# A static order for one TensorE-bound program laid out again, with other transfer constants and one more wait in its planner

## The chip, the cores and the metric

The kernel runs on one core of a Trainium2 chip. The metric is the device time in microseconds (us) of one execution; the kernel before has a median of 942.45 us over three runs (941.67 to 943.02). Five engines run their own instruction lists in order: TensorE (PE), VectorE (DVE), ScalarE (ACT), GpSimd (POOL) and SyncE (SP, which here only issues transfers).

## What is computed

Random-feature attention over 8 batches, 8 heads, 576 positions and 64 channels with 128 features, followed by a layer norm and a two-layer perceptron (512 to 2048 to 512) with a residual:

```python
def phi(x):
    proj = np.einsum('bhsd,md->bhsm', x, omega)
    h = proj - np.sum(x * x, axis=-1, keepdims=True) / 2.0
    return np.exp(h - np.max(h, axis=-1, keepdims=True)) / np.sqrt(m)
q_p, k_p = phi(q * scale), phi(k * scale)
kv = np.einsum('bhsm,bhsd->bhmd', k_p, v)
z = np.sum(k_p, axis=2)
x = np.einsum('bhsm,bhmd->bhsd', q_p, kv) / (np.einsum('bhsm,bhm->bhs', q_p, z)[..., None] + 1e-06)
# x as rows of 512, then
xn = (x - mu) / np.sqrt(var + 1e-06) * g_ln
out = x + np.maximum(xn @ w_ch1, 0.0) @ w_ch2
```

## The kernel before

**Tiles.** The 8 x 576 positions are 4608 rows, cut into 36 chunks of 128 rows (`c`) and 9 tiles of 512 rows (`t`, four chunks each). Tiles 0 to 2 go through the perceptron plainly: `mm1` (L1085 to L1087) makes one of 16 blocks `f` of the hidden layer, `relu` evicts it into a high and a low part, `mm2` (L1128 to L1130) adds it to four result banks. Each product is three matmuls, high by high, low by high and high by low. Tiles 3 to 8 are three pairs `p`. For a pair the first layer is done with seven products instead of eight on quarters of the operands: `one_set` (L1429 to L1431) makes two blocks of the hidden layer for both tiles in seven products; between them ACT copies a partial sum from bank to bank (`gen_copy`, L1486) or into `hid` (`gen_snap`, L1492), and DVE adds (L1499, L1507). After two sets `one_chunk` (L1748 to L1750) does the second layer for eight chunks, and DVE drains each result bank into `x` (`drain`, L1767). In the last pair the second layer has seven products too (`two_chunks`, `product2`, L1668 to L1670); their operands are made by `form_a11`, `form_a21`, `form_a12`, `form_s4` and `form_sum`.

**Attention** runs in the gaps of that stream as short visits on PE: `gen_k` (L663, features of keys), `gen_sums` (L726, keys by values), `gen_q` (L824, and L841/L842 from chunk 8 on, features of queries), `gen_x` (L907, the output). For a query chunk from 8 on, SP loads `qD` (L829), ACT makes the high part (L834), DVE the low part (L836), PE multiplies (L841, L842), ACT or DVE copies out (L369, L371), POOL takes the maximum over partitions (L853), DVE subtracts it (L858), ACT takes the exponential (L861). For keys, `gen_v` loads `v` and DVE sets its column of ones when it has landed (L622). A chunk of `x` is normalised (L991 or L993), split into halves (L1008), transposed by a transfer (L1011) and copied in place (L369 or L371). `gen_rs` makes the row scale of a tile from its statistics with small instructions on DVE (L963, L971 to L977) and ACT (L967, L969).

**Order.** Nothing is decided on the chip. At build time `Plan.run` picks the next piece of work for each engine by its own estimate of when it can start, and by rank; the order in which it picks is the order in which each engine's instructions are written. Its estimates rest on constants: a transfer lands `FLIGHT` (1.8 us) after its issue or after the one ahead of it, whichever is later, plus its bytes at 400 GB/s; a transposing transfer (`"flip"`) takes `FLOWN` more; `MARGIN` is added to what ACT or DVE take over from another engine; during the first part of a maximum on POOL, DVE instructions marked `"two"` (two operands in SBUF) are held back from `EDGE[0]` before to `EDGE[1]` after a window of 1.9 us. `EDGE` and `MARGIN` count only after `TILL` (60 us). `SHIFT` moves the rank of single pieces, `WAIT` and `SOLO` say when a lone visit is let onto PE, `EARLIER`, `WF`, `W2F` set base ranks. Semaphores for every true dependence are put in by the framework, whatever the order.

In the last pair, bank `b_b` is read twice: by ACT, and then DVE, in `form_a12` (L1595, L1597), and by DVE in `form_s4` (L1609).

Of the kernel before, what the change touches and what calls it, by code (L numbers as in the profile page):

```python
# [1957 lines left out]
```

## Time and profile before

| | |
|---|---|
| median of 3 runs | 942.45 us |
| the profiled execution | 943.46 us |
| its span, first to last instruction | 941.7 us |
| PE busy | 925.3 us (98%) |
| DVE busy | 677.3 us (72%) |
| ACT busy | 503.4 us (53%) |
| POOL busy | 123.3 us (13%) |
| granted TensorE clock | 1.0 throughout |
| DMA queues, share of 16 engines | 65%, 215 GB/s on average |

The profiled execution took 943.46 us; 1.8 us of it lie outside the span, and it is 1.0 us above the median. A timeline row has start, duration, engine, line, operation and tiles; in brackets stands how long the engine was idle ahead of it, and what ended that. A row such as `DMA quad<-qD` among the waits means that the engine waited for a transfer's landing.

### The profile page before, as it was taken

The numbers are of one execution on the slowest core, as the hardware profiler recorded it, in microseconds if no ns is written. First come the engines' busy times: TensorE is split into PE (matmuls) and PEld (weight loads), VectorE is DVE, ScalarE is ACT, GpSimd is POOL, SyncE is SP. The second block draws the span as 40 slices with busy tenths as digits, with TensorE's granted clock in tenths as the row PEclk, the third lists the DMA queues.
The fourth block names the chain that finished last, engine by engine and source line by source line (L and its number), as shares of the span: only waits on it lengthen the run. The fifth ranks groups of instructions, "written<-read, shape, count | busy, mean of one in ns | idle before, by whom it ended". The sixth has DMA issues, their size and how long they took to land.

```text
span 941.7 us, 17585 instructions
## 1 busy us (share of the span) xinstructions
PE 925.3 (98%) x6863; PEld 767.1 (81%) x6863; DVE 677.3 (72%) x1176; ACT 503.4 (53%) x919; POOL 123.3 (13%) x47
## 2 busy tenths in 40 slices
PE   8999999999999999999999999999999999999998
PEld 6887778788888878887787888887888888989988
DVE  6999999565588865546664668797837496585765
ACT  6888886454665654334545556656513245263442
POOL 5002304100303350000410111404000000000000
PEclk9999999999999999999999999999999999999999
DMA  8576599964456955575766664695937468484562
GB/s 306 203 264 230 162 332 397 340 203 131 143 184 205 202 144 203 181 261 176 245 152 208 171 211 156 218 379 124 330 120 260 168 214 303 163 293 125 189 224 90
DMA packets 142579, 202.72 MB, mean 215 GB/s; under 512 B 44064, under 2 KB 79008, under 8 KB 142496
## 3 DMA queue, kind: packets, MB, share of 16 engines
q1 hardware_dynamic: 142352, 201.34, 65.0%
q8 instruction: 54, 0.88, 0.4%
q10 hardware_dynamic: 144, 0.26, 0.1%
q14 instruction: 29, 0.24, 0.1%
HBM read 140.74 MB, written 52.43 MB: 205 GB/s over the span
## 4 chain that ended last, share of the span: by engine, by line
PE 52%; DMA 6%; DVE 4%; ACT 2%; issue 1%; SPq 0%; DVEq 0%; ACTq 0%
PE b L1429 7%; PE b L1431 7%; PE b L1430 7%; PE b L1748 5%; PE b L1750 5%; PE b L1749 5%; PE b L1668 2%; PE b L1670 2%; PE b L1669 2%; DMA quad<-qD 2%; PE b L726 1%; PE b L907 1%; PE b L663 1%; PE b L1130 1%; PE b L1128 1%
## 5 line engine op out<-in xcount | busy, mean ns | idle before, releaser
L853 POOL PARTITION_ALL_REDUCE quad<-quad x34 | 117.1, 3463 | 528.6 <-ACT quad L369 321.3
L1429 PE MATMUL b<-w,w 128*128 128x512 f32 x336 | 132.2, 393 | 1.8 <-ACT hid L1492 1.0
L1430 PE MATMUL b<-w,w 128*128 128x512 f32 x336 | 130.8, 389 | 0.0
L1431 PE MATMUL b<-w,w 128*128 128x512 f32 x336 | 130.8, 389 | 0.0
L1748 PE MATMUL b<-w,w 128*128 128x512 f32 x256 | 101.5, 396 | 1.1 <-DVE x L1767 1.1
L1750 PE MATMUL b<-w,w 128*128 128x512 f32 x256 | 99.9, 390 | 0.9 <-DVE w L1517 0.9
L1749 PE MATMUL b<-w,w 128*128 128x512 f32 x256 | 99.8, 390 | 0.0
L672 ACT ACTIVATE kp<-b,mb 128x128 f32<-128x128 f32 x256 | 70.3, 391 | 42.3 <-DVE mb L666 40.4
L1085 PE MATMUL b<-xnT,w 128*128 128x512 f32 (+1 forms) x200 | 78.6, 393 | 0.0
L1128 PE MATMUL b<-w,hid 128*128 128x512 f32 x192 | 77.8, 405 | 0.5 <-ACT hid L1101 0.5
L1087 PE MATMUL b<-xnT,w 128*128 128x512 f32 (+1 forms) x200 | 76.4, 382 | 0.5 <-DVE xnT L1061 0.4
L1429 PEld LDWEIGHTS b<-w,w 128*128 128x128 f32 x336 | 63.0, 188 | 16.9 <-ACT b L1486 2.1
L1086 PE MATMUL b<-xnT,w 128*128 128x512 f32 (+1 forms) x200 | 76.3, 382 | 0.2 <-DVE w L580 0.2
L1130 PE MATMUL b<-w,hid 128*128 128x512 f32 x192 | 75.0, 391 | 0.0
L1129 PE MATMUL b<-w,hid 128*128 128x512 f32 x192 | 75.0, 390 | 0.0
L1431 PEld LDWEIGHTS b<-w,w 128*128 128x128 f32 x336 | 63.1, 188 | 13.3
L1492 ACT COPY hid<-b 128x512 f32<-128x512 f32 x64 | 37.6, 587 | 67.0 <-PE b L1431 37.2
L1430 PEld LDWEIGHTS b<-w,w 128*128 128x128 f32 x336 | 63.1, 188 | 12.6
L1499 DVE TENSOR_TENSOR b<-b,hid 128x512 f32<-128x512 f32 x32 | 22.3, 697 | 63.6 <-ACT hid L1492 63.6
L1486 ACT COPY b<-b 128x512 f32<-128x512 f32 x32 | 18.4, 577 | 89.4 <-PE b L1431 68.3
L1748 PEld LDWEIGHTS b<-w,w 128*128 128x128 f32 x256 | 48.0, 188 | 13.0 <-DVE x L1767 2.2
L1750 PEld LDWEIGHTS b<-w,w 128*128 128x128 f32 x256 | 48.0, 188 | 11.5 <-DVE w L1517 1.3
(224 smaller groups left out, 2045.5 us busy)
## 6 DMA issues: line engine op xcount, KB each, us to landing
w<-wf SPq DMA_DIRECT2D x168, 256.0 KB, 4.8
w<-w SPq DMA_DIRECT2D x32, 512.0 KB, 6.2
w<-w2a SPq DMA_DIRECT2D x32, 512.0 KB, 5.4
quad<-qD SPq DMA_DIRECT2D x28, 512.0 KB, 4.8
w2a<-w SPq DMA_DIRECT2D x16, 512.0 KB, 5.6
wf<-wide SPq DMA_DIRECT2D x32, 256.0 KB, 3.2
w2t<-wide SPq DMA_DIRECT2D x32, 256.0 KB, 3.9
away<-x SPq DMA_DIRECT2D x30, 256.0 KB, 3.5
```

What stands on the lines that cost most here:

```text
L853: nc.gpsimd.partition_all_reduce(mx.rearrange("p a b -> p (a b)"), qc.rearrange("p a b -> p (a b)"), P, bass_isa.ReduceOp.max)
L1085: nc.tensor.matmul(ph[:, ts], w[:, 0, cs], xnT[:, 0, k, ts], start=k + i0 == 0, stop=False)
L1086: nc.tensor.matmul(ph[:, ts], w[:, 1, cs], xnT[:, 0, k, ts], start=False, stop=False)
L1087: nc.tensor.matmul(ph[:, ts], w[:, 0, cs], xnT[:, 1, k, ts], start=False, stop=k == NK - 1 and i1 == TC)
L1128: nc.tensor.matmul(accs[i][:, c], hl[:, 0, cs], w[:, 0, c], start=(f == 0), stop=False)
L1130: nc.tensor.matmul(accs[i][:, c], hl[:, 1, cs], w[:, 0, c], start=False, stop=f == NF - 1 and c == parts[-1])
L1429: nc.tensor.matmul(o, w[:, 0, cs], hi[:, k], start=first and k == 0, stop=False, skip_group_check=True)
L1430: nc.tensor.matmul(o, w[:, 1, cs], hi[:, k], start=False, stop=False, skip_group_check=True)
L1431: nc.tensor.matmul(o, w[:, 0, cs], lo[:, k], start=False, stop=k == 1, skip_group_check=True)
L1748: nc.tensor.matmul(acc[:, o], hl[:, 0, cs], w[:, 0, o], start=n == 0 and o is parts[0], stop=False)
L1749: nc.tensor.matmul(acc[:, o], hl[:, 0, cs], w[:, 1, o], start=False, stop=False)
L1750: nc.tensor.matmul(acc[:, o], hl[:, 1, cs], w[:, 0, o], start=False, stop=n == 3 and o is parts[-1])
```

## The change

Four things in the planner and one wait. A transfer issued after 60 us is reckoned to land 0.5 us later, at 1/1.11 of the rate. `FLOWN` goes from 2.2 to 1.2, `EDGE` from (0.5, 0.2) to (0.1, 0.1), ACT's `MARGIN` from 0.15 to 0.2. `SHIFT` is another table (entries for the same kinds of pieces with other numbers), and `W2F`, `WAIT`, `SOLO`, `EARLIER`, `WF` have other values. `form_s4` waits, in the plan, until `form_a12` has issued ACT's read of the bank.

```diff
-                self.dma_at = max(self.dma_at, start + Plan.FLIGHT) + cost * (1.55 if self.dma_at < Plan.SLOW else 1.0)
+                late = start > Plan.TILL
+                self.dma_at = max(self.dma_at, start + Plan.FLIGHT + 0.5 * late) + cost * (1.55 if self.dma_at < Plan.SLOW else 1.11 if late else 1.0)
...
         nc.scalar.activation(out=hl[:, 0], in_=bank(b_b), func=AF.Relu)
+        done(("a12", j))
...
         yield wait("f", j, "S2")
+        yield wait("a12", j)
         s4 = yield from whole(j, "S4")
...
-SHIFT = {('gen_w2store', 13): 4, ('gen_q', 26): 12, ('gen_var', 28): -18, ...
+SHIFT = {('gen_var', 16): -2, ('gen_w2store', 13): 12, ('gen_q', 26): 12, ...
-W2F = -40
-WAIT = (0, 0, 24)
-SOLO = (0, 0, 0)
+W2F = -30
+WAIT = (-2, -6, 23)
+SOLO = (2, 9, 5)
...
-MARGIN = {ACT: 0.15, DVE: 0.15}
-FLOWN, EDGE = 2.2, (0.5, 0.2)
+MARGIN = {ACT: 0.2, DVE: 0.15}
+FLOWN, EDGE = 1.2, (0.1, 0.1)
...
-EARLIER = {2: 1.8, 3: 2.25, 4: 2.5, 5: 3.95, 6: 6.6, 7: 5.75, 8: 5.3}
+EARLIER = {2: 1.25, 3: 2.2, 4: 2.7, 5: 3.6, 6: 6.8, 7: 5.65, 8: 3.95}
...
-WF = (44, 12.75)
+WF = (35, 15.0)
```

PE's main stream (the three perceptron parts) stands in the same order in both programs, and so does its whole start up to the visit of `gen_sums` for batch 1 behind block 7 of tile 0. Between there and the last pair the attention's visits stand at other places of that stream; in the last pair PE, DVE and ACT have the same rows. Lines of the changed kernel are 1 to 3 higher than those of before.

**First pair, DVE.** The ones of the `v` of batch 6, chunk 2 (MEMSET on `v_`), with the maxima of two key chunks ahead (L666 TENSOR_REDUCE) and a drain behind (L1767). Before:

```order
L836 TENSOR_TENSOR quad_4619<-quad_4600,quad_4619 64x1024
L666 TENSOR_REDUCE mb_4604<-b 128x8
L666 TENSOR_REDUCE mb_4566<-b 128x8
L622 MEMSET v_4680 128x8
L1767 SCALAR_TENSOR_TENSOR x_4423<-b,st_3543,x_4423 128x512
```

Now:

```order
L667 TENSOR_REDUCE mb_4345<-b 128x8
L667 TENSOR_REDUCE mb_4331<-b 128x8
L837 TENSOR_TENSOR quad_4584<-quad_4564,quad_4584 64x1024
L837 TENSOR_TENSOR quad_4593<-quad_4581,quad_4593 64x1024
L1770 SCALAR_TENSOR_TENSOR x_4475<-b,st_2549,x_4475 128x512
L623 MEMSET v_4621 128x8
```

Two low parts of queries and a drain have moved between the maxima and the MEMSET.

**First pair, ACT.** The high part of query chunk 25 (`quad_4850` before, `quad_4746` now) and the copies of `one_set` (COPY b<-b, and COPY of `hid` at L1492, now L1493). Before:

```order
L1486 COPY b<-b 128x512
L1008 COPY wide_4868<-wide_4857 128x1024
L369 COPY quad_4866<-b 128x1024
L834 CAST quad_4850<-quad_4838 128x1024
L1492 COPY hid_4251<-b 128x512
```

Now, chunk 25 first and, some rows later, chunk 26 (`quad_4940`):

```order
L835 CAST quad_4746<-quad_4735 128x1024
L370 COPY xnT_4436<-wide_4785 128x2x4x128
L673 ACTIVATE kp_4717<-b,mb_4718 128x128 x4
L370 COPY xnT_4436<-wide_4802 128x2x4x128
L673 ACTIVATE kp_4717<-b,mb_4718 128x128 x4
```

```order
L1516 ACTIVATE w_30_4992<-b 128x512
L970 ACTIVATE w_150_4365<-w_150_4365 128x4
L835 CAST quad_4940<-quad_4930 128x1024
L1487 COPY b<-b 128x512
L862 ACTIVATE quad_4958<-quad_4958 128x1024
```

Chunk 25's CAST has moved out of the set into the chunks of the second layer; chunk 26's stands directly ahead of a copy between banks.

**Second pair, DVE.** The low parts of query chunks 34 and 35 (`quad_6534`, `quad_6545` before) and the row scale's small instructions on `st_`. Before:

```order
L836 TENSOR_TENSOR quad_6534<-quad_6513,quad_6534 64x1024
L1767 SCALAR_TENSOR_TENSOR x_6399<-b,w_150_4245,x_6399 128x512
L963 TENSOR_SCALAR st_6068<-st_6068 128x4
L971 TENSOR_TENSOR st_6068<-st_6068 128x4
L836 TENSOR_TENSOR quad_6545<-quad_6530,quad_6545 64x1024
```

Now:

```order
L964 TENSOR_SCALAR st_6115<-st_6115 128x4
L1770 SCALAR_TENSOR_TENSOR x_6391<-b,w_150_4365,x_6391 128x512
L837 TENSOR_TENSOR quad_6523<-quad_6502,quad_6523 64x1024
L837 TENSOR_TENSOR quad_6533<-quad_6519,quad_6533 64x1024
L1770 SCALAR_TENSOR_TENSOR x_6404<-b,w_150_4365,x_6404 128x512
L972 TENSOR_TENSOR st_6115<-st_6115 128x4
```

The instruction that takes ACT's result (L971, now L972) has moved behind both low parts and a drain.

**Last pair, SP.** The loads of weights into `kv` and `v` for `product2` and the loads of chunks of `x` (L945, now L946, from `away`). Before:

```order
L1651 DMA v_7715<-w2t_114 128x512
L945 DMA w_140_4228<-away_6405 128x512
L1359 DMA w_20_3550<-wf_91 128x512
L1649 DMA v_7716<-w2a_98 128x2x256
L945 DMA x_7865<-away_6748 128x512
L1359 DMA w_20_3550<-wf_92 128x512
L1649 DMA v_7717<-w2a_100 128x2x256
L945 DMA x_7878<-away_6812 128x512
```

Now:

```order
L1654 DMA v_7716<-w2t_114 128x512
L1360 DMA w_20_3554<-wf_91 128x512
L1652 DMA v_7717<-w2a_98 128x2x256
L1360 DMA w_20_3554<-wf_92 128x512
L1652 DMA v_7718<-w2a_100 128x2x256
L946 DMA x_7838<-away_6563 128x512
L946 DMA x_7852<-away_6393 128x512
L946 DMA w_140_4342<-away_6731 128x512
```

Three loads of `x` have moved behind the last load into `v`.

## Rows read from the trace of the kernel before

**Rows 1.** The page: PE's busy time, and its commonest matmul with mean duration.

```profile
PE 925.3 (98%) x6863; PEld 767.1 (81%) x6863; DVE 677.3 (72%) x1176; ACT 503.4 (53%) x919; POOL 123.3 (13%) x47
...
L1430 PE MATMUL b<-w,w 128*128 128x512 f32 x336 | 130.8, 389 | 0.0
```

**Rows 2.** PE's waits, longest first: us in total, times, longest; first and last.

```profile
PE b L841 <- DVE quad L836: 2.2, 2, 1.8
...
PE b L663 <- DVE hid L1103: 0.2, 1, 0.2
```

**Rows 3.** Waits of ACT and DVE for transfers, same columns.

```profile
ACT quad L834 <- DMA quad<-qD: 20.1, 9, 5.2
...
DVE v L622 <- DMA v<-vF: 14.1, 7, 4.6
```

**Rows 4.** Timeline, first pair, around 437 us.

```profile
431.23 0.34 SPq L618 DMA_DIRECT2D v<-vF  x1
...
436.72 0.07 DVE L622 MEMSET v<- 128x8 f32 x1 [2.55 <-DMA v<-vF]
...
437.62 0.50 PE L1748 MATMUL b<-w,w 128*128 128x512 f32 x1 [1.06 <-DVE x L1767]
```

**Rows 5.** Timeline, first pair, 451 to 462 us.

```profile
451.08 0.43 SPq L829 DMA_DIRECT2D quad<-qD  x1
...
458.15 1.05 ACT L834 CAST quad<-quad 128x1024 fp32r<-128x1024 f32 x1 [2.69 <-DMA quad<-qD]
459.11 0.58 ACT L1492 COPY hid<-b 128x512 f32<-128x512 f32 x1
...
459.74 0.50 PE L1429 MATMUL b<-w,w 128*128 128x512 f32 x1 [1.01 <-ACT hid L1492]
...
461.82 0.47 PE L841 MATMUL b<-quad,om_hi 128*128 128x512 f32 x1 [0.43 <-DVE quad L836]
```

**Rows 6.** Timeline, first pair, 465 to 469 us, while POOL takes a maximum.

```profile
465.18 0.68 DVE L1517 SCALAR_TENSOR_TENSOR w<-b,w 128x512 fp32r<-128x512 f32 x1
...
465.96 2.47 DVE L1517 SCALAR_TENSOR_TENSOR w<-hid,w 128x512 fp32r<-128x512 f32 x1
...
469.09 0.51 PE L1750 MATMUL b<-w,w 128*128 128x512 f32 x1 [0.86 <-DVE w L1517]
```

**Rows 7.** Timeline, second pair, 638 to 643 us.

```profile
638.31 1.03 ACT L834 CAST quad<-quad 128x1024 fp32r<-128x1024 f32 x1
...
640.43 0.20 ACT L969 ACTIVATE st<-st 128x4 f32<-128x4 f32 x1
...
640.67 0.16 DVE L971 TENSOR_TENSOR st<-st 128x4 f32<-128x4 f32 x1 [1.80 <-ACT st L969]
640.86 1.22 DVE L836 TENSOR_TENSOR quad<-quad,quad 64x1024 fp32r<-64x1024 f32 x1
...
642.23 0.47 PE L841 MATMUL b<-quad,om_hi 128*128 128x512 f32 x1 [1.77 <-DVE quad L836]
```

**Rows 8.** Timeline, last pair, a load into `v` and its matmul.

```profile
803.39 0.53 SPq L1649 DMA_DIRECT2D v<-w2a  x1
...
808.69 0.38 PE L1668 MATMUL b<-v,w 128*128 128x256 f32 x1 [0.43 <-DMA v<-w2a]
```

**Rows 9.** Timeline, last pair, the two readers of bank `b_b`, second of eight times.

```profile
798.99 0.60 ACT L1595 ACTIVATE w<-b 128x512 fp32r<-128x512 f32 x1 [0.76 <-PE b L1431]
...
800.80 0.68 DVE L1609 SCALAR_TENSOR_TENSOR wide<-b,wide 128x512 f32<-128x512 f32 x1
```

**Rows 10.** View of the transfers: count, median us from issue to landing.

```profile
wide<-wide SPq DMA_TRANSPOSE x32, 4.3
```

**Rows 11.** Timeline of the start: two DVE instructions and PE's first wait in the perceptron.

```profile
27.48 0.41 DVE L371 CAST w<-wide 128x512 fp32r<-128x512 f32 x1
...
32.07 0.68 DVE L564 TENSOR_TENSOR wide<-wide,g_sb 128x512 f32<-128x512 f32 x1
...
38.30 0.39 PE L1087 MATMUL b<-xnT,w 128*128 128x256 f32 x1 [0.43 <-DVE xnT L1061]
```

More of the change, by code (lines that the diff above doesn't have):

```diff
@@ L1886 @@
 MOST_URGENT = -2000
-SHIFT = {('gen_w2store', 13): 4, ('gen_q', 26): 12, ('gen_var', 28): -18, ('gen_var', 15): -30, ('gen_sums', 6, 1): 26, ('gen_q', 16): -36, ('gen_x', 26): 20, ('gen_q', 7): -8, ('gen_var', 33): 12, ('gen_q', 4): 2, ('gen_k', 3, 3): -8, ('gen_x', 7): -8, ('gen_q', 30): 28, ('gen_sums', 3, 2): -8, ('gen_x', 35): -10, ('gen_sums', 0, 2): -40, ('gen_x', 29): 2, ('gen_q', 34): 34, ('gen_q', 18): 4, ('gen_w2store', 12): -12, ('gen_wform', 5): -4, ('gen_w2store', 14): -6, ('gen_q', 33): 16, ('gen_var', 17): 16, ('gen_x', 21): -2, ('gen_q', 24): -2, ('gen_q', 14): -2, ('gen_q', 10): 0, ('gen_sums', 4, 2): -2, ('gen_x', 1): 0, ('gen_x', 15): -24, ('gen_var', 8): 12, ('gen_w2store', 2): -4, ('gen_q', 15): 4, ('gen_var', 10): 40, ('gen_x', 13): 8, ('gen_var', 7): -6, ('gen_var', 13): -32, ('gen_var', 21): 16, ('gen_x', 6): -14, ('gen_k', 3, 2): 2, ('gen_w2store', 1): 4, ('gen_x', 3): 14, ('gen_k', 2, 4): -2, ('gen_sums', 6, 2): 12, ('gen_var', 23): 4, ('gen_sums', 0, 1): -8, ('gen_sums', 0, 0): 16, ('gen_sums', 7, 1): -16, ('gen_var', 5): 4, ('gen_q', 35): 0, ('gen_q', 27): 16, ('gen_var', 3): 8, ('gen_x', 23): -8, ('gen_q', 22): 2, ('gen_w2store', 9): 2, ('gen_q', 9): 4, ('gen_k', 4, 1): 16, ('gen_var', 31): -16, ('gen_k', 5, 4): 16, ('gen_x', 31): -4, ('gen_q', 11): -16, ('gen_k', 3, 4): 8, ('gen_q', 28): 16, ('gen_k', 7, 2): 2, ('gen_var', 6): -12, ('gen_k', 6, 0): -4, ('gen_k', 6, 1): 8, ('gen_x', 30): -2, ('gen_k', 4, 4): -4, ('gen_sums', 4, 0): -16, ('gen_q', 29): 12, ('gen_k', 6, 4): 2, ('gen_x', 34): -16, ('gen_q', 31): 4, ('gen_w2store', 11): 16, ('gen_w2store', 0): 4, ('gen_k', 6, 3): 8, ('gen_wform', 0): -2, ('gen_w2store', 7): -8, ('gen_x', 24): 0, ('gen_var', 19): 16, ('gen_var', 14): -18, ('gen_sums', 7, 0): -8, ('gen_x', 8): 2, ('gen_var', 32): -4, ('gen_w2store', 10): -16, ('gen_k', 7, 1): 8, ('gen_k', 5, 0): 2, ('gen_q', 17): 2, ('gen_x', 10): -2, ('gen_wform', 1): -2, ('gen_x', 11): 16, ('gen_k', 0, 4): 4, ('gen_sums', 2, 1): -2, ('gen_w2store', 8): 4, ('gen_w', 1, 0): -2, ('gen_q', 32): 8, ('gen_k', 4, 3): -16, ('gen_k', 5, 3): 8, ('gen_k', 2, 3): 16, ('gen_q', 23): 2, ('gen_var', 1): -8, ('gen_w2store', 3): -8, ('gen_k', 7, 0): 4, ('gen_var', 34): -16, ('gen_var', 9): 16, ('gen_x', 16): 8, ('gen_var', 27): 2, ('gen_var', 22): -8, ('gen_k', 0, 0): -16, ('gen_sums', 6, 0): 16, ('gen_sums', 1, 2): -16, ('gen_x', 19): 2, ('gen_var', 11): -16, ('gen_var', 2): -16, ('gen_var', 12): 8}
@@ L1888 @@
-W2F = -40
-WAIT = (0, 0, 24)
-SOLO = (0, 0, 0)
+SHIFT = {('gen_var', 16): -2, ('gen_w2store', 13): 12, ('gen_q', 26): 12, ('gen_var', 28): 2, ('gen_var', 15): -14, ('gen_sums', 6, 1): 28, ('gen_q', 16): -36, ('gen_x', 26): 20, ('gen_q', 7): -8, ('gen_var', 33): 16, ('gen_k', 3, 3): 0, ('gen_x', 7): -8, ('gen_sums', 3, 2): -4, ('gen_x', 35): -10, ('gen_x', 29): 2, ('gen_w2store', 12): -20, ('gen_w2store', 14): -6, ('gen_q', 33): 20, ('gen_var', 17): 16, ('gen_x', 21): -2, ('gen_q', 24): -2, ('gen_q', 14): -2, ('gen_q', 10): 0, ('gen_x', 1): 0, ('gen_x', 15): -24, ('gen_w2store', 2): -4, ('gen_q', 15): 4, ('gen_x', 5): -12, ('gen_var', 10): 40, ('gen_var', 7): -6, ('gen_x', 6): -16, ('gen_k', 3, 2): 2, ('gen_w2store', 1): 4, ('gen_k', 2, 4): 2, ('gen_sums', 6, 2): 4, ('gen_var', 23): 4, ('gen_sums', 0, 0): 20, ('gen_sums', 7, 1): -20, ('gen_var', 5): 4, ('gen_q', 27): 16, ('gen_var', 3): 6, ('gen_x', 23): -6, ('gen_q', 22): 2, ('gen_var', 31): -24, ('gen_k', 5, 4): 16, ('gen_x', 31): -6, ('gen_q', 11): -32, ('gen_k', 7, 2): 2, ('gen_var', 6): -12, ('gen_k', 6, 1): 12, ('gen_x', 30): -4, ('gen_w2store', 4): -16, ('gen_sums', 4, 0): -16, ('gen_q', 29): 12, ('gen_k', 6, 4): -14, ('gen_x', 34): -20, ('gen_w2store', 11): 18, ('gen_w2store', 0): 4, ('gen_wform', 0): -10, ('gen_x', 24): -16, ('gen_var', 19): 28, ('gen_sums', 7, 0): -24, ('gen_x', 8): 2, ('gen_var', 32): -20, ('gen_w2store', 10): -16, ('gen_q', 17): 2, ('gen_x', 10): -2, ('gen_wform', 1): 12, ('gen_k', 0, 4): 4, ('gen_sums', 2, 1): -2, ('gen_w2store', 8): 4, ('gen_k', 5, 3): -6, ('gen_q', 8): -8, ('gen_q', 20): 2, ('gen_q', 25): 6, ('gen_x', 32): -8, ('gen_var', 2): 16, ('gen_k', 5, 2): 4, ('gen_sums', 3, 0): -8, ('gen_q', 3): -2, ('gen_x', 9): -2, ('gen_q', 21): 16, ('gen_wform', 7): 16, ('gen_x', 17): -4, ('gen_q', 32): -20, ('gen_k', 7, 3): -4, ('gen_w2store', 3): -8, ('gen_sums', 6, 0): -4, ('gen_k', 3, 1): -4, ('gen_sums', 1, 2): -10, ('gen_wform', 2): -2, ('gen_wform', 4): 18, ('gen_w2store', 5): 2, ('gen_w2store', 6): 10, ('gen_sums', 1, 1): -2, ('gen_var', 26): 4, ('gen_q', 19): 8, ('gen_var', 1): -2, ('gen_sums', 0, 1): -24, ('gen_var', 29): 20, ('gen_w', 2, 0): -2, ('gen_x', 20): 16, ('gen_k', 4, 3): 2, ('gen_sums', 2, 2): -4, ('gen_sums', 7, 2): 16, ('gen_q', 23): -4, ('gen_w', 2, 15): 2, ('gen_wform', 3): -8, ('gen_k', 6, 2): 8, ('gen_var', 21): 16, ('gen_q', 18): -16, ('gen_wform', 6): -8, ('gen_var', 0): 4, ('gen_var', 22): -2}
```

## Prediction

> **What bounds the kernel now.** I read the page first. PE is busy 925.3 of the span's 941.7 us [rows 1], and the clock is granted in full throughout, so the program is PE's stream, and a change can gain only by what PE waits or by what it runs beside its products. The order shows that the second is unchanged: the same matmuls, and as many places where the main stream stops for visits (63 groups of attention visits with narrow matmuls and 28 query visits with full-width ones, before and now). That leaves the waits: 16.4 us of the span. The list of PE's waits has fifteen lines that add up to 11.7 us, from 2.2 to 0.2 [rows 2]; 3.4 of them (1.6, 1.2, 0.4 and 0.2) fall in the first 40 us, where PE's order stays, so **8.3 us** of waits are open to the new order. The rest of the 16.4 us is the first microsecond and the drains and stores behind the last matmul, which have the same rows now. A wait costs a little more than its gap: the first matmul behind it takes 0.50 us [rows 4, 5], against a mean of 0.389 [rows 1], so some 0.1 us each.
>
> Then I looked for who makes PE wait. It is rarely a long queue of work: it is ACT or DVE, held in its own list by a transfer that lands later than the plan thought. ACT waited 20.1 us for loads of queries and DVE 14.1 us for loads of `v` [rows 3], and most of that cost PE nothing. It cost something where an eviction that PE needs stood right behind.
>
> **The change part by part.** All sums are made on the profiled execution (943.46 us) and then set off from the median, 942.45.
>
> *Visits.* Their number is equal, each visit's matmuls too. 0 us.
>
> *The wait for the bank's first reader.* It adds no instruction. In all eight cases DVE's read (L1609) starts some 1.2 us after ACT's read has ended (800.80 against 798.99 + 0.60) [rows 9], and DVE's and ACT's rows in the last pair are the same as before. Nobody queues behind it for longer. 0 us, in both directions.
>
> *The `v` of batch 6, chunk 2.* Its load is issued at 431.23, DVE reaches the MEMSET after the two maxima and is idle 2.55 us; the drain behind it comes late and PE waits 1.06 us for the bank [rows 4]. Now two low parts (1.22 us each, as in rows 7) and a drain stand between: about 3.2 us more than the idle 2.55. The wait goes, unless the load too has moved back as far: -1.1 us, bounds -1.2 and 0.
>
> *Query chunk 25.* The load is issued at 451.08 and lands 7 us later; ACT is held 2.69 us at L834, the copy that `one_set` needs comes at 459.11, PE waits 1.01 us at 459.74 and 0.43 us more for the low part at 461.82 [rows 5]. Now that CAST stands in the chunks of the second layer with no copy of a set near behind it, where a late ACT delays transposes and keys, not PE's banks. -1.4 us, bounds -1.6 and 0. But chunk 26's CAST stands right ahead of a copy between banks now. It is priced below.
>
> *Query chunks 34 and 35.* DVE's L971 takes ACT's result L969, and ACT runs that behind a CAST and a copy: DVE is idle 1.80 us, though the high part that the second L836 needs was done at 639.34 (638.31 + 1.03). L836 starts at 640.86 and PE waits 1.77 us, the longest wait of all [rows 7]. With L971 behind both low parts, L836 can start at about 639.5, 1.4 us earlier. What is late next is ACT's CAST itself, held in its turn behind a normalisation (L991) that needs a free buffer. So -1.4 us and not the whole 1.77; bounds -1.9 and 0.
>
> *The last loads of the last pair.* The load into `v` is issued at 803.39 and lands just late: PE waits 0.43 us [rows 8]. An issue takes SP 0.53 us there, so three that moved behind it bring it forward by some 1.6 us. The three loads of `x` that are late instead are read by drains of the second group, many products on. -0.4 us, bounds -0.6 and 0.
>
> *Guard around POOL's maximum.* A DVE instruction with two operands in SBUF that meets the start of a maximum took 2.47 us where the same with one in a bank took 0.68, and PE waited 0.86 us for it [rows 6]. The new order has the maximum elsewhere, but the plan's margin ahead of it has shrunk from 0.5 to 0.1 us. I take half of the wait as gone, -0.4, bounds -1.0 and +1.9 (two new ones of that size). The Trainium skill (GPSIMD Engine Reference, section 8, Key points) says that POOL shares its SBUF interfaces with VectorE, in contention with DVE instructions in a two-port mode or with two SBUF inputs. Rows 6 agree with it. By that rule alone the narrower margin is a loss: the last rival below.
>
> *The other waits.* 8.3 less those five places (1.1, 1.4, 1.8, 0.4, 0.9) leaves 2.7 us in small waits elsewhere, for low parts of queries, evictions and weights. Their places are written in another order throughout. Transfers are reckoned 0.5 us later and about a tenth slower, which puts their takers further back; the shares that DVE backlog caused stay. Half: -1.3 us, bounds -2.7 and 0.
>
> *Restarts.* Some six waits fewer in net, 0.1 us each: -0.6.
>
> *What comes new.* An order with as many takers of transfers will hold some at a bad place: (1) chunk 26's CAST ahead of a copy between banks, price as in [rows 5], 1.0; (2) a MEMSET for `v` ahead of a drain, price as in [rows 4], 1.1; (3) takers of transposes: the plan's whole allowance for one went from 1.8 + 0.9 + 2.2 = 4.9 us to 1.8 + 0.5 + 1.0 + 1.2 = 4.5, while the median from issue to landing is 4.3 [rows 10], so a good part of them come later than that. I take two such waits, +2.1; bounds 0 and +6.
>
> *The start.* Ahead of the first transposed tile, DVE now multiplies by the gain (L564, 0.68 us) where it cast before (L371, 0.41 us), and PE waits for DVE's result (0.43 us at 38.30) [rows 11]: +0.3, bounds 0 and +0.6.
>
> The sum: -1.1 - 1.4 - 1.4 - 0.4 - 0.4 - 1.3 - 0.6 + 2.1 + 0.3 = **-4.2 us**. The profiled execution would come to 939.3, the median to **938.3**.
>
> **Rivals.**
>
> *All goes well.* Every wait behind 40 us goes (-8.3, and -1.2 of restarts) with new ones of no more than 1 us: 942.45 - 8.5 = 934.0. For it: the changed constants are those by which the known waits came about. Against it: some waits are for DVE's own backlog (677.3 us of work [rows 1]), which no constant shortens.
>
> *Waits only change places.* The new order has other takers at bad places and gains within 1.9 us: about 941.5. For it: the old order too was made to have no waits by its own plan, and has 8.3 us. Against it: four of the named waits have a cause that the order rows show moved.
>
> *Slower.* DVE instructions with two SBUF operands are caught by the starts of maxima, because the margin ahead is 0.1 us. There are 28 maxima behind 60 us, one for each query chunk from 8 on. A caught instruction costs DVE 1.8 us (2.47 against 0.68) and, where PE needs what stands behind, PE 0.86 and 0.1 of a restart [rows 6]. From seven such waits on, the gain of 4.2 is more than gone and the kernel slower: 942.45 - 4.2 + 7 x 0.96 = 945.0. For it: the guard is narrower by 0.5 us in all. Against it: in the trace of before only one of PE's waits is of this kind. This is the rule of the skill's page, carried to its end.
>
> **How the numbers follow.** About 0.2% (1.9 us) is what a measurement of this kernel can tell from no change. The forecast, a gain of 2 to 8.5 us: 0.66. All goes well and more: 0.06. Waits only change places, or the start and new waits eat the gain: 0.20. Slower by any mechanism: 0.08, of which the guard has 0.05. Faster is 0.66 + 0.06 = 0.72. The forecast's own range is 934.0 to 940.5. To hold the time 8 times in 10 the range must reach over most of the second rival: 934.0 to 943.3 leaves out 0.06 below, 0.08 above and some 0.05 of the equal cases.
>
> **What would show it.** In the profile after, PE's matmul groups keep count and mean. The five waits named are gone from PE's list: DVE's L837 for the later of chunks 34 and 35 starts within 0.3 us of the end of its CAST on ACT; no L623 in the first pair has an idle of more than 1 us directly ahead of a drain; the last load into `v` lands before its matmul. The sum of PE's waits for lines behind 40 us falls from 8.3 to 4 or 5. DVE's and ACT's waits for loads of `v` and queries fall from 34.2 us together to below 25. It is wrong if PE's waits stay at 8 with other names, if DVE instructions of 2 us or more behind POOL's starts stand ahead of PE's waits, or if PE's first product starts later than 34 us by more than the 0.3.

## The result, and the profile after

The changed kernel takes **931.82 us** (median of 4 runs, 931.34 to 932.3), against 942.74 for the kernel before on the same chip: a ratio of 0.9881, 95% interval 0.9862 to 0.9900, some 11 us less. The forecast was 938.3 with a range from 934.0; the time lies below it. Five more runs on another chip gave 931.58 and a ratio of 0.9864 (0.9843 to 0.9886).

Line numbers of the changed kernel are those of before plus 1 to 3 (L834 is L835, L836 is L837, L1429 is L1430, L1748 is L1751). The profiled execution took 932.1 us with a span of 930.3. From its page, the busy times and the chain of work that ended last:

```profile
PE 921.4 (99%) x6863; PEld 768.1 (83%) x6863; DVE 677.0 (73%) x1180; ACT 501.5 (54%) x914; POOL 118.5 (13%) x47
...
PE 94%; DVE 2%; DMA 2%; issue 0%; ACT 0%; SPq 0%; DVEq 0%
```

Against [rows 1] the span is 11.4 us shorter. PE's idle time went from 16.4 (941.7 - 925.3) to 8.9 us (930.3 - 921.4), 7.5 us of it; the other 3.9 us left PE's *busy* time, with the same 6863 matmuls. DVE and ACT have nearly the same work as before. PE's waits, whole list (us in total, times, longest), which answers to [rows 2]:

```profile
PE b L825 <- ACT kp L690: 1.4, 1, 1.4
PE b L496 <- DVE spin L455: 1.2, 1, 1.2
PE b L1086 <- ACT xnT L1060: 0.7, 1, 0.7
PE b L842 <- DVE kv L755: 0.4, 1, 0.4
PE b L1088 <- DVE xnT L1062: 0.4, 1, 0.4
PE b L825 <- ACT quad L370: 0.2, 1, 0.2
```

Six lines instead of fifteen. Behind 40 us there is one wait left, 0.4 us at 153 us, where there were 8.3 us; no line of before has its pair of names, so it is a new one. The two at L1086 and L1088 are at 38 and 39 us, in the start; the first of them is new. The takers of transfers, which answer to [rows 3], and the landing times of the same loads in the view of the transfers:

```profile
ACT quad L835 <- DMA quad<-qD: 8.8, 6, 5.7
```
```profile
DVE v L623 <- DMA v<-vF: 3.0, 1, 3.0
```
```profile
quad<-qD SPq DMA_DIRECT2D x28, 512.0 KB, 4.8
...
v<-vF SPq DMA_DIRECT2D x28, 260.0 KB, 3.6
...
wide<-wide SPq DMA_TRANSPOSE x32, 3.4
```

These loads are no quicker: in the kernel before the median was 4.8 us for the queries too and 3.3 us for `v`. (The transposes are: 3.4 us where [rows 10] have 4.3.) The takers wait less because they stand further back: from the issue of a query's load to the start of its CAST the median went from 6.0 to 6.4 us, and 7 of the 28 CASTs start within 0.1 us of the landing where 11 did (counted in the two traces). And where one still waits, nobody on PE needs what is behind it; the timelines of ACT and of DVE (start, duration, idle ahead in brackets) have the two longest:

```profile
416.29 1.05 ACT L835 CAST quad<-quad 128x1024 fp32r<-128x1024 f32 x1 [5.66 <-DMA quad<-qD]
417.56 1.04 ACT L835 CAST quad<-quad 128x1024 fp32r<-128x1024 f32 x1 [0.21 <-DMA quad<-qD]
420.02 4.33 ACT L673 ACTIVATE kp<-b,mb 128x128 f32<-128x128 f32 x16 [1.42 <-DVE mb L667]
```
```profile
230.92 0.07 DVE L623 MEMSET v<- 128x8 f32 x1 [3.00 <-DMA v<-vF]
```

### The profile page after: what moved, and what is told of

It reads as the page before. It is cut to its first block, busy times and chain, and to the rows that moved or that the text cites. A ratio compares the mean times of both kernels' runs of the same rounds, so it can differ in the third digit from the quotient of the medians.

```text
span 930.3 us, 17558 instructions
## 1 busy us (share of the span) xinstructions
PE 921.4 (99%) x6863; PEld 768.1 (83%) x6863; DVE 677.0 (73%) x1180; ACT 501.5 (54%) x914; POOL 118.5 (13%) x47
## 4 chain that ended last, share of the span: by engine, by line
PE 94%; DVE 2%; DMA 2%; issue 0%; ACT 0%; SPq 0%; DVEq 0%
PE b L1430 8%; PE b L1432 8%; PE b L1431 8%; PE b L1751 7%; PE b L1753 6%; PE b L1752 6%; PE b L1129 5%; PE b L1086 5%; PE b L1088 5%; PE b L1087 5%; PE b L1130 5%; PE b L1131 5%; PE b L908 4%; PE b L727 3%; PE b L664 3%; PE b L1673 3%
## 5 line engine op out<-in xcount | busy, mean ns | idle before, releaser
L854 POOL PARTITION_ALL_REDUCE quad<-quad x34 | 112.3, 3321 | 521.3 <-ACT quad L370 271.9
L1430 PE MATMUL b<-w,w 128*128 128x512 f32 x336 | 131.8, 392 | 0.0
L1751 PE MATMUL b<-w,w 128*128 128x512 f32 x256 | 101.2, 395 | 0.0
L1086 PE MATMUL b<-xnT,w 128*128 128x512 f32 (+1 forms) x200 | 78.1, 391 | 0.7 <-ACT xnT L1060 0.7
L1088 PE MATMUL b<-xnT,w 128*128 128x512 f32 (+1 forms) x200 | 76.4, 382 | 0.5 <-DVE xnT L1062 0.4
L1430 PEld LDWEIGHTS b<-w,w 128*128 128x128 f32 x336 | 63.0, 188 | 14.0 <-ACT b L1487 0.9
L1432 PEld LDWEIGHTS b<-w,w 128*128 128x128 f32 x336 | 63.1, 188 | 13.3
L1493 ACT COPY hid<-b 128x512 f32<-128x512 f32 x64 | 37.5, 586 | 67.8 <-PE b L1432 37.8
L1431 PEld LDWEIGHTS b<-w,w 128*128 128x128 f32 x336 | 63.1, 188 | 12.7
L1104 DVE SCALAR_TENSOR_TENSOR hid<-b,hid 128x512 fp32r<-128x512 f32 x48 | 33.0, 688 | 37.9 <-ACT hid L1102 37.4
L1751 PEld LDWEIGHTS b<-w,w 128*128 128x128 f32 x256 | 48.0, 188 | 10.8
```

What stands on the lines that cost most here:

```text
L1086: nc.tensor.matmul(ph[:, ts], w[:, 0, cs], xnT[:, 0, k, ts], start=k + i0 == 0, stop=False)
L1088: nc.tensor.matmul(ph[:, ts], w[:, 0, cs], xnT[:, 1, k, ts], start=False, stop=k == NK - 1 and i1 == TC)
L1430: nc.tensor.matmul(o, w[:, 0, cs], hi[:, k], start=first and k == 0, stop=False, skip_group_check=True)
L1431: nc.tensor.matmul(o, w[:, 1, cs], hi[:, k], start=False, stop=False, skip_group_check=True)
L1432: nc.tensor.matmul(o, w[:, 0, cs], lo[:, k], start=False, stop=k == 1, skip_group_check=True)
L1751: nc.tensor.matmul(acc[:, o], hl[:, 0, cs], w[:, 0, o], start=n == 0 and o is parts[0], stop=False)
```

## The experiments

Times of a run are compared with runs of the kernel before on the same chip (943.5 to 944.7 us there); a gain in us is what the ratio lacks to 1, times that.

**One place at a time in the kernel before.** Each edit adds one wait to the plan, so that one row (in e4 three, in the last pair four SP rows) moves and all else keeps its order. e1 has all four:

```diff
+        if t == 7:
+            yield wait("low", 35)
...
+        if (b, c) == (6, 2):
+            yield wait("drained", 17, 0)
...
+        if c in (31, 32, 33):
+            yield wait("go3", 0, 13)
...
+            if c == 25:
+                yield wait("snap", 0, 3, 0)
```

They stand, in this order, ahead of L971 (`gen_rs`), the MEMSET of `v`, the last pair's loads of `x`, and ACT's copy of the query.

> The kernel before, with only the order at four of the prediction's places written anew (4 DVE or ACT rows and the last pair's SP loads move, the constants and ranks stay): L971 behind the low part of chunk 35, the MEMSET of v (batch 6, chunk 2) behind the drain of chunk 17, the last pair's loads of x of chunks 31 to 33 behind the load into v, query chunk 25's copy behind the copy between banks that held PE. Theory A (a wait costs its listed gap and 0.27 us more, because a matmul's row lasts 0.39 us where starts lie 0.23 apart, and the first one behind a wait is 0.11 longer; and nothing else is late next): the five gaps 1.77, 1.06, 1.01, 0.43 and 0.43 leave PE's list, 4.7 + 5 x 0.27 = 6.1 us less, 936.6. Theory B (the steps of the prediction, which held back part of each for what is late next): -4.3 and -0.5 for restarts, 937.9. Rival (what is removed is given back at the next late transfer): PE's list keeps 6 us or more behind 40 us under other names, and the time falls by less than 2 us, 941 or more.

Measured: 939.9 us (6 runs), ratio 0.9956 (0.9941 to 0.9970), 4.2 us less (2.8 to 5.6). Lines of PE's waits:

```profile
PE b L846 <- ACT quad L369: 2.1, 2, 1.2
...
PE b L1759 <- DVE w L1526: 1.2, 1, 1.2
...
PE b L1137 <- ACT hid L1110: 0.9, 1, 0.9
PE b L1438 <- ACT hid L1501: 0.4, 1, 0.4
```

The waits at 437, 460, 462 and 808 us are gone. The one at 642 us is not: it is now the 1.2 us at L846, for another eviction. Theory A's 6.1 us is out, since at 642 us something else was late next; B's 4.8 is near, and the rival's "under 2 us" is out.

> The kernel before, with one DVE row moved: L971 of the last tile stands behind both low parts of query chunks 34 and 35. Theory A (whole gap and 0.27 us): the wait of 1.77 us at L841 near 642 us is gone, -2.0 us, 940.4. Theory B (the prediction's step: ACT's CAST is late next and keeps 0.4 us of it): a wait of some 0.4 us stays at the same matmul, -1.5 us, 941.0. Rival (given back): a new wait of over 1 us within the next 20 us, time as before.

Measured: 942.68 us (10 runs), ratio 0.9980 (0.9967 to 0.9994), 1.9 us less (0.6 to 3.1). From ACT's and DVE's timelines, which answer to [rows 7]:

```profile
638.20 1.04 ACT L834 CAST quad<-quad 128x1024 fp32r<-128x1024 f32 x1
639.14 1.03 ACT L1011 COPY wide<-wide 128x1024 uint16<-128x1024 uint16 x1
...
640.43 0.99 ACT L369 COPY quad<-b 128x1024 f32<-128x1024 f32 x1
```
```profile
639.27 1.22 DVE L836 TENSOR_TENSOR quad<-quad,quad 64x1024 fp32r<-64x1024 f32 x1 [0.52 <-ACT quad L834]
```

DVE's L836 starts 0.03 us behind the CAST that it needs (638.20 + 1.04), at 639.27 where it was 640.86. PE still waits 1.18 us, until L369's end: ACT evicts its other bank behind the copy L1011. Of 1.77 us only 0.6 went. Both A (all of it) and B (0.4 us left) fall by PE's list, which the time cannot tell apart: 0.6 us is the lower end of the measured interval, and waits that the edit does not touch spread by as much (below).

> The kernel before, with one DVE row moved: the MEMSET that waits for the load of v (batch 6, chunk 2) stands behind the drain of chunk 17. Theory A: the wait of 1.06 us at L1748 near 437 us is gone and DVE still waits some 1.9 us for the load, behind the drain, without anyone on PE noticing: -1.3 us, 941.1. Rival (a late load is paid wherever its taker stands): DVE's wait moves to the low part or drain behind it, a wait of 0.5 us or more opens on PE within 20 us, and the time is within 0.5 us of before.

Measured: 942.03 us (10 runs), ratio 0.9977 (0.9966 to 0.9989), 2.2 us less (1.0 to 3.2). PE's wait at 437 us is gone and none within 20 us takes its place: theory A, and its 1.3 us lies in the interval. This execution's load came earlier, too: DVE waited 0.41 us for it, not 2.55 [rows 4].

> The kernel before, with ACT's copy of query chunk 25 (L834, the taker of a load that lands 7 us after its issue) put behind the copy between banks (L1492); one other copy changes from DVE to ACT and one PE row moves. Theory A: the waits of 1.01 and 0.43 us at L1429 and L841 near 460 us are gone, -1.44 - 0.54 = -2.0 us, 940.5. Theory B (the prediction's step): -1.4 - 0.2 = -1.6 us. Rival (the low part, L841, is as late as before, since the load's landing sets it): only the 1.01 goes and L841's wait grows to some 1 us; time within 0.7 us of before.

Measured: 942.75 us (10 runs), ratio 0.9989 (0.9972 to 1.0006): 1.0 us less, from 2.6 less to 0.6 more. Both gaps at 460 us are gone from PE's list, as A has it; the old one behind them, at 469 us, is 1.4 us in this execution where it was 0.9, which is in the spread of such places (last section). The time alone would not have told.

**Constants against ranks.** The diff has two halves, and each was run alone: e5 has the constants, e6 the ranks (`SHIFT`, `W2F`, `WAIT`, `SOLO`, `EARLIER`, `WF`), both on the kernel before. Of e5:

```diff
+                late = start > Plan.TILL
+                self.dma_at = max(self.dma_at, start + Plan.FLIGHT + 0.5 * late) + cost * (1.55 if self.dma_at < Plan.SLOW else 1.11 if late else 1.0)
...
+MARGIN = {ACT: 0.2, DVE: 0.15}
+FLOWN, EDGE = 1.2, (0.1, 0.1)
```

> The kernel before with the new constants alone (transfers 0.5 us later and 1.11 times as long, MARGIN, FLOWN, EDGE); ranks (SHIFT, W2F, WAIT, SOLO, EARLIER, WF) as before. Theory C (the constants do it: a plan that knows when loads land puts every taker behind its landing, whatever the ranks): DVE's and ACT's waits for loads fall as in the changed kernel (L622 3 us, L834 9 us, from 14 and 20), PE's waits behind 40 us fall from 8.3 to under 2, 934 or less. Rival T (the ranks were laid out for the constants; alone neither helps): PE's waits stay at 6 us or more, with two more places where the main stream stops, 941 or more. In between, by parts: half of the waits, 938.

> The kernel before with the new ranks alone; constants as before. Theory C: transfers are planned as early as before, L622 and L834 wait as before (14 and 20 us), PE's waits behind 40 us stay at 6 to 10 us, 940 to 944. Rival R (the ranks do it, by moving the known takers from their bad places): PE's waits fall under 3 us, 935 or less. Rival T: 941 or more, as theory C, so that this run parts R from the two others and the run of the constants alone parts C from T.

Measured: constants alone 955.43 us, ratio 1.0111 (1.0064 to 1.0159); ranks alone 966.31 us, ratio 1.0236 (1.0191 to 1.0281). (The added wait in `form_s4` is in neither half; in the last pair, where it stands, the rows of PE, DVE and ACT did not change.) Each half is slower than the kernel before, and both together are 11 us faster: rival T. C and R are out. But e5's windows (length, then busy time of PE, PEld, DVE, ACT, POOL, the granted clock, DMA share, GB/s) show what the constants do:

```profile
300.00:360.00 60.00, 60.00 (x476) 49.22 (x475) 41.48 (x74) 34.92 (x51) 20.31 (x6) 1.00 0.55 166
360.00:388.00 28.00, 28.00 (x146) 22.81 (x145) 15.09 (x26) 14.29 (x24) 6.45 (x2) 1.00 0.83 257
388.00:440.00 52.00, 37.81 (x363) 28.07 (x363) 39.67 (x75) 32.15 (x63) 6.99 (x2) 0.84 0.67 204
440.00:500.00 60.00, 60.00 (x475) 49.96 (x474) 29.71 (x49) 26.55 (x58) 3.22 (x1) 1.00 0.67 211
```

PE stands still in one stretch of 52 us, where the second layer's product begins, and in no window from 60 to 860 us outside it; the kernel before has twelve waits behind 40 us, from 101 to 809. The plan of e5 itself lets PE idle in that stretch: 22.7 us of its 23.7 us of idle time behind 40 us lie there. In the one stretch the chain runs through ACT and DVE, which still have attention work of the last tiles to do, while the split of the layer's first operand (L1312) stands behind it. That is a question of which work comes first, so of ranks. In e6 the waits are spread: 7.7 us at 158 to 164 us, 2.1 at 473, 2.1 at 647, 7.5 at 791 to 812. Those at 473 and 647 us (and 0.9 at 359) are at places where the plan has PE busy.

**The parts of the constants.** e7 takes the lateness out of the changed kernel, e8 puts `FLOWN` back; e9 adds the lateness alone to the kernel before; e10 empties `SHIFT` in the changed kernel; e11 and e12 keep one half of the lateness each:

```diff
 e8  -FLOWN, EDGE = 1.2, (0.1, 0.1)
 e8  +FLOWN, EDGE = 2.2, (0.1, 0.1)
 e10 +SHIFT = {}
 e11 -start + Plan.FLIGHT + 0.5 * late
 e11 +start + Plan.FLIGHT
 e12 -1.11 if late else 1.0
 e12 +1.0
```

> The changed kernel without its later and slower transfers (0.5 us and 1.11 taken out; MARGIN, FLOWN, EDGE and the ranks stay). Theory C in its narrow form (it is the lateness of transfers that takes PE's waits away): waits of L622 and L834 return to some 30 us together, PE's waits behind 40 us return to 5 us or more, 938 or more. Rival T (ranks tuned to the whole set): the same, 938 or more, since the order is another throughout; the two differ in where PE waits: by C for evictions behind takers of loads, by T for anything. Rival M (margins and FLOWN matter, not the lateness): under 934.

> The changed kernel with FLOWN put back to 2.2 (takers of transposes planned 1.0 us further behind their loads); everything else as changed. The prediction feared that the shorter allowance brings waits of ACT and DVE for transposes that land later than planned, two of PE's at 1 us each. Theory C (the lateness already covers it; the allowance of 1.2 costs nothing): no gain, 932 to 934. Rival T (any other constant spoils the fit of the ranks): PE's waits behind 40 us come back to 3 us or more, 936 or more.

> The kernel before with later and slower transfers alone (0.5 us, 1.11); MARGIN, FLOWN, EDGE and the ranks as before. The planner keeps a clock of its own while it writes the order; at its last PE step that clock stands at 925.2 us for the kernel before, 925.9 for the changed kernel, 949.7 with the constants alone, 948.0 with the ranks alone, 975.7 without the lateness, 984.8 with the old FLOWN. The measured spans (941.7, 930.3, 953.4, 968.4, 994.6, 987.2) stand 16.5, 4.4, 3.7, 20.4, 18.9 and 2.4 above it. Theory P (two separate things: the ranks set the plan's end, the lateness alone sets how far the chip falls behind the plan): here the plan ends at 973.8, so the span is 976 to 979 and the time 978 to 981. Rival Q (FLOWN, EDGE and MARGIN close part of the 16.5): 8 us or more behind the plan, time 984 or more. Rival C (late transfers help whatever the plan says): under 942.

> The changed kernel with an empty SHIFT; constants and the other ranks as changed. The plan ends at 957.8. Theory P: 2 to 5 us behind the plan, 962 to 965. Rival S (the table was chosen with the chip's own waits in view, so that another order under the same constants has new waits): 10 us or more behind the plan, 970 or more, with PE's waits spread over the program as in the kernel before.

> The changed kernel with transfers 1.11 times as long but not 0.5 us later; everything else as changed. The plan ends at 963.8. Theory P with the fixed part as the cause (a load of 256 KB is reckoned at 0.66 us, so 1.11 adds 0.07 us to one and some 0.6 to a queue of eight, less than the waits of before): 12 to 17 us behind the plan, 978 to 983. With the rate as the cause (loads come in bursts): 3 to 7 us behind, 969 to 973.

> The changed kernel with transfers 0.5 us later but not 1.11 times as long; everything else as changed. The plan ends at 935.6. Theory P with the fixed part as the cause: 4 to 7 us behind the plan, 941 to 944. With the rate as the cause: 12 to 17 us behind, 949 to 955.

Measured, with the planner's own clock at its last PE step (`free_at[PE]`, a number of the program that writes the order, not of the chip) beside the measured span. "Idle in plan" is what the plan itself lets PE wait behind 40 us. Time is a median, span and granted clock are of the profiled execution:

| kernel | time, us | plan's end | idle in plan | span | span less plan | clock |
|---|---|---|---|---|---|---|
| before (no lateness) | 943.5 | 925.2 | 1.4 | 941.7 | 16.5 | 1.000 |
| e6, ranks alone (none) | 966.3 | 948.0 | 24.5 | 968.4 | 20.4 | 0.982 |
| e7, changed less the lateness (none) | 996.4 | 975.7 | 48.5 | 994.6 | 18.9 | 0.974 |
| e12, 0.5 us alone | 946.3 | 935.6 | 9.0 | 943.1 | 7.5 | 0.998 |
| e11, 1.11 alone | 969.0 | 963.8 | 37.2 | 966.2 | 2.4 | 0.985 |
| e9, lateness alone on before | 974.8 | 973.8 | 46.9 | 972.7 | -1.1 | 0.985 |
| e8, changed with the old `FLOWN` | 989.0 | 984.8 | 60.1 | 987.2 | 2.4 | 0.972 |
| e5, constants alone | 955.4 | 949.7 | 23.7 | 953.4 | 3.7 | 0.991 |
| e10, changed with an empty `SHIFT` | 970.9 | 957.8 | 32.3 | 969.0 | 11.2 | 0.981 |
| changed | 931.8 | 925.9 | 1.9 | 930.3 | 4.4 | 0.999 |

(e6 was profiled in its slowest execution and e12 in its fastest; the medians of their spans are 964.6 and 944.5, which stand 16.6 and 8.9 us above the plan.)

Without the lateness the chip falls 16 to 20 us behind its plan; with both halves of it, 4.4 us or less in four of five orders. The ranks decide where the plan itself ends, and every constant or rank altered alone here puts the plan's end 10 to 59 us later: e8 is 57 us slower than the changed kernel, and 58.9 us of that stand in its plan already. So e8 answers to rival T, with 30.7 us of PE's waits back, and e7's 996 us to both C and T, which it does not part; M is out.

Theory P, that the lateness alone sets how far the chip falls behind, came out only roughly. e9 was to end 2 to 5 us behind its plan and ended 1.1 us ahead of it, nearer to P than to Q and C but outside P's range. e11, at 2.4, is at the edge of P's version with the rate as the cause (3 to 7); e12 lies between the two versions (4 to 7, 12 to 17), nearer the one with the fixed part. By the column alone the rate does more (2.4 us behind against 7.5), but neither half is shown to be the cause. e10 came 11.2 us behind where P had 2 to 5; that and its time meet rival S's figures (10 or more, 970 or more), so S, that the table was chosen with the chip's own waits in view, stands untested.

The column is also no clean measure of late loads. Where the plan lets PE idle, a late load can cost nothing. And in all orders with much idle time the granted clock fell: in e10, 29 starts of wide matmuls with no listed wait ahead lie 0.42 to 0.62 us apart instead of 0.227, 7.0 us in all, which is as much as the 7 us by which it missed P; in e8, 13.4 us of the same kind leave it only 2.4 behind. So the rows with next to no idle time in the plan, before and changed, are the fair pair: 16.5 against 4.4. The plan's end moved by 0.7 us, the wrong way, so the whole gain in span lies in the distance to the plan. These two differ in all constants and in the order; the runs show that the scattered waits go under the new constants as a set (e5), not that the lateness alone takes them away.

**The start.** In the changed kernel ACT's L541 waits 1.04 us for a weight, and the copy of the fourth transposed tile (L1060) stands behind it. e13 is the changed kernel again; e14 and e15 put the tile's two rows ahead without touching the plan, by handing in the others' instructions later:

```diff
+            put = (lambda e, op: later[e].append(op)) if (n, f) in ((1, 3), (2, 1)) else lambda e, op: op()
...
+        if (t, i) == (0, 3):
+            for op in later[ACT]:
+                op()
```

> The changed kernel, unaltered, as the partner of the next run on the same chip. Its PE list should again have no wait of more than 0.5 us behind 40 us (both theories).

> The changed kernel with two ACT and two DVE rows of the start put behind the copy and the subtraction of the fourth transposed tile (in the changed kernel they stand ahead of these, and the first of them waits 1.04 us for a weight load at 36.53); no other row of any engine moves, the planner's order stays. Theory W (a listed gap costs its length and some 0.27 us more): PE's gaps of 0.67 and 0.39 us at 38.29 and 39.18 go, 1.06 + 0.54 = 1.6 us below the partner run. Rival L (a listed gap costs its length alone): 1.1 us below. Rival G (the weights that the moved rows prepare come later and PE waits for them instead): a new gap of 0.5 us or more at 39 to 50 us, within 0.5 us of the partner.

Measured: e13 931.58 us, e14 935.49 (ratio 0.9909, 0.9888 to 0.9929). The two gaps went, but e14's scaling of the same weights (L376) also moved ahead of DVE's row that reads them, which then waited; from DVE's and PE's timelines:

```profile
38.34 1.29 DVE L545 SCALAR_TENSOR_TENSOR w<-w,wide 128x512 uint32<-128x512 uint32 x2 [1.60 <-ACT w L376]
```
```profile
40.88 0.50 PE L1137 MATMUL b<-w,hid 128*128 128x512 f32 x1 [1.18 <-ACT hid L1110]
42.69 0.79 PE L1139 MATMUL b<-w,hid 128*128 128x512 f32 x1 [1.08 <-DVE hid L1112]
```

An edit that does more than it says; it tells nothing of the two gaps' price. Its 3.9 us over e13 are more than its waits: PE's listed waits grew by 1.3 us (4.2 to 5.6), and from 43.29 to 45.42 us, behind the second new wait, the wide matmuls start 0.43 us apart where 0.23 is usual. The windows from 33 to 60 us (columns as above), of e14 and then of e13, show the clock:

```profile
33.00:60.00 27.00, 24.63 (x135) 20.38 (x134) 24.67 (x43) 20.26 (x38) 0.00 (x0) 0.94 0.68 239
```
```profile
33.00:60.00 27.00, 26.04 (x148) 21.76 (x146) 26.32 (x49) 21.91 (x44) 0.00 (x0) 1.00 0.76 268
```

e15 leaves the scaling in its place:

> The changed kernel with the copy (ACT) and the subtraction (DVE) of the fourth transposed tile each put ahead of the two rows that stood before them; unlike the run before, the scaling of the same two weights stays behind DVE's rows, so no other row moves against its neighbours. Theory W (a listed gap costs its length and some 0.27 us): PE's gaps of 0.67 and 0.39 us at 38 to 39 us go, the two of 1.18 and 1.08 us that the run before opened at 41 and 43 us do not come, 931.7 - 1.6 = 930.1. Rival L (gap alone): 930.6. Rival G (the weights come later by the two rows' 1.2 us and PE waits for them instead): gaps of 0.5 us or more at 40 to 50 us, 931 to 933.

Measured, on a third chip: 931.19 us (5 runs), ratio 0.9863 (0.9836 to 0.9889), span 929.4. PE's waits behind 33 us, of e13 and then of e15:

```profile
PE b L1086 <- ACT xnT L1060: 0.5, 1, 0.5
PE b L842 <- DVE kv L755: 0.5, 1, 0.5
PE b L1088 <- DVE xnT L1062: 0.4, 1, 0.4
PE b L1430 <- ACT hid L1493: 0.3, 1, 0.3
```
```profile
PE b L1141 <- DVE hid L1114: 0.8, 1, 0.8
PE b L845 <- DVE kv L758: 0.5, 1, 0.5
```

The two gaps are gone and one of 0.8 us has come at 41 us, rival G in part. The listed waits fell by 0.3 us (1.6 to 1.3, rounded as the view gives them) and by two in number, the span by 0.9 us: 0.3 + 2 x 0.27 = 0.8 by theory W, 0.3 by rival L. This does not part W from L: the five spans of e13 alone run from 928.7 to 930.3, and the medians of the spans, 929.7 and 929.4, differ by 0.3. In the median time e15 is 0.4 to 0.6 us below the changed kernel, less than these measurements tell apart.

## Why the prediction was too high

**What bounds the kernel** held: PE's stream is the time, the matmuls and visits are the same, and only waits changed. All five named places are free of waits, and the last pair has none, so the wait for the bank's first reader cost nothing there. What failed is four terms of the sum. Between the two profiled executions it was to be -4.2 us and was -11.4:

| term | taken, us | measured, us |
|---|---|---|
| the five places | -4.7 | -5.6 |
| the other waits | -1.3 | -2.7 |
| restarts (what a wait costs beyond its gap) | -0.6 | -3.9 |
| what comes new | +2.1 | +0.4 |
| the start | +0.3 | +0.5 |

The measured terms add up to -11.3. The largest misses are the restarts (3.3 us) and what comes new (1.7).

**The price of a wait was too small**, and this was the largest miss. I took the listed gap and 0.1 us for the longer first matmul. But a row of a wide matmul lasts 0.39 us where the starts in an undisturbed row of them lie 0.227 us apart (worked out from PE's start times), so the first 0.16 us of a gap hide under the modelled end of the row before. A wait costs its gap + 0.16 + 0.11 us. Between wide matmuls, before had twelve intervals longer than usual by over 0.15 us, 9.3 us in all, the changed kernel one of 0.6. Eleven waits fewer at 0.27 are 3.0 of the 3.9 us that left PE's busy time. The other 0.9 are stalls too short to be listed: three of the twelve intervals (0.39, 0.43 and 0.43 us, at 175, 177 and 647 us) show no wait in PE's list, and hold 0.6 us over the usual and the longer matmul three times.

**"The other waits: half" was too little.** 2.7 us were reckoned to go by half; all went. The argument against, that some of these waits are DVE's own backlog which no constant shortens, did not hold: the order is written from the start with the landings as reckoned, and e5 shows that under the new constants no wait of PE is left outside one stretch.

**"What comes new: +2.1"** came as one wait of 0.4 us, and no load is behind it: DVE, which ends it with L755, is busy without a gap from 147 us on, and the plan itself lets PE idle 0.9 us there. Late takers are there, as reckoned: chunks' copies that wait 5.66 and 1.62 us, a MEMSET 3.00. None stands ahead of an eviction that PE needs. The row tells a waiter; it took the row behind it to tell a cost, and I priced new waiters without that row. Nor do the transposes that land later than the plan's 4.5 us (11 of 32, 13 before) cost PE anything: ACT's waits for them fell from 7.1 to 3.8 us.

**Chunks 34 and 35**: mechanism right, cure wrong. e2 freed L836 as told, and 1.18 us of the wait stayed, behind ACT's L1011. The step named ACT as late next and still took 1.4. In the changed kernel both CASTs are done before DVE gets to the pair's second half, and PE does not wait. The sign that I gave, L837 within 0.3 us of its CAST's end, did not come: the later one starts 0.9 us behind, since the two stand together. From ACT's and DVE's timelines:

```profile
625.92 1.06 ACT L835 CAST quad<-quad 128x1024 fp32r<-128x1024 f32 x1 [0.29 <-DMA quad<-qD]
627.29 1.05 ACT L835 CAST quad<-quad 128x1024 fp32r<-128x1024 f32 x1 [0.32 <-DMA quad<-qD]
```
```profile
628.13 2.36 DVE L837 TENSOR_TENSOR quad<-quad,quad 64x1024 fp32r<-64x1024 f32 x2
```

**The last pair's loads**: the wait at 808 went, as told. The sentence that the three later loads of `x` are read only in the second group was wrong: one is read in the first, and DVE waited for it, at no cost to PE:

```profile
798.15 0.48 DVE L1725 SCALAR_TENSOR_TENSOR x<-hid,st,x 128x256 f32<-128x256 f32 x1 [1.40 <-DMA x<-away]
```

**The guard around POOL's maximum**: half of 0.86 was taken, all of it went. The narrower margin does let DVE's rows be caught, here in DVE's and POOL's timelines:

```profile
454.52 1.97 DVE L1518 SCALAR_TENSOR_TENSOR w<-hid,w 128x512 fp32r<-128x512 f32 x1 [0.54 <-ACT w L1516]
```
```profile
454.05 3.22 POOL L854 PARTITION_ALL_REDUCE quad<-quad  x1 [3.55 <-DVE w L964]
```

With [rows 6]: 2.47 there, 1.97 here, 0.68 where it is free. That agrees with the rule of the Trainium skill (GPSIMD Engine Reference, section 8, Key points) cited in the prediction. But DVE's rows that are 0.9 us or more longer than the median of their kind went from seventeen to twelve, and no PE wait follows from one. (Behind 60 us POOL runs 32 maxima in either trace, not 28.) The rival "slower" fell on its second condition, that PE needs what is caught.

**The start**: +0.3 taken for L564's 0.68 us; the first product starts 0.09 us later (33.59 against 33.50; 32.97 in e13, the same program), so that row's cost does not show. What cost was the order three rows on: a CAST that PE needs behind a row that waits for a weight. The start's listed waits went from 3.4 to 3.9 us (3.5 in e13).

**The chances.** The rival "all goes well" had 0.06 and is what happened. I weighed it by the waits that I could explain one by one. The better question is how far the chip falls behind the order's own reckoning, 16.5 us, and whether the change takes away the error behind it. The sum of places came out near where it named them (e1: 4.2 us measured, 4.8 expected), in part by luck: 1.2 us of wait stayed at 642 us that the step had let go to 0.4, and each wait that went was worth more than I took. It was too small for the whole change because the new constants and ranks together took nearly every wait away, not only the named ones.

## What to carry to other kernels

Where an order is laid out by a plan, correct the plan's transfer times by the trace first and lay the ranks out anew after; a constant or a rank table altered alone in such a kernel cost 14 to 65 us here and says nothing about its own worth. A late load costs what stands behind its taker, not what the taker waits: look for the eviction in the next row. When pricing PE's waits, add to each listed gap what the modelled end of the matmul before hides, here 0.16 us, and the longer first matmul, 0.11.
